# Agent attention and a tanh MLP on one core: the first keys with 49 agent columns, one weight quarter decoded later, two quarters split by ScalarE

## The chip, the cores and the metric

The kernel runs on one core of a Trainium2 chip. The metric is the device time of one execution in microseconds (us), lower is better. The core has TensorE (PE in the profile, with its weight loads as PEld), VectorE (DVE), ScalarE (ACT), GpSimd (POOL) and SyncE (SP), whose queue issues the DMAs here. Each works off its own instructions in order and waits for the others by semaphores.

## The reference

Per batch (4 batches, 12480 tokens, 128 channels) 49 agents attend to the keys and values, then the queries attend to the agents; the result goes through one MLP with `h - tanh(h)` between its two weights.

```python
def sm(a, b):
    s = scale * (a @ b.transpose(0, 2, 1))
    s = s - s.max(-1, keepdims=True)
    e = np.exp(s)
    return e / (e.sum(-1, keepdims=True) + 1e-09)
agent_v = sm(agents, k) @ v          # 49 x 128 per batch
x = sm(q, agents) @ agent_v          # 49920 x 128 in all
h = x @ w_in                         # w_in 128 x 2048
out = (h - np.tanh(h)) @ w_out       # w_out 2048 x 128
```

w_in and w_out come as float64; the kernel takes their bits as integers and makes float32 of them itself.

## The kernel before, in words

**Stages.** The 49920 tokens are cut into 100 blocks of 500, and each block passes eight steps (`HP = 8`, two 128-row chunks of the 2048 inner rows a step). One step is a first product `m1` (L563, into a PSUM tile `h`), `tanh` and `square` on ScalarE (L573, L578), the product `g` on VectorE (L583) and the second product `m2` (L632, into `acc`). For the 800 steps TensorE is the busy engine. In block 0 every step is "plain": `m2` multiplies by the float32 weights `wf` as they were decoded. From the third step of block 1 on most steps split `g` into a rounded part (GpSimd, L613) and a rest (VectorE, L618), and use W_out split in the same way, `wo_h` and `wo_l`.

**The opening** is what comes before block 0, and it is for batch 0 alone (`phase1(0)`; the other batches' attention is done between the steps of the blocks). In this order:

1. *Scores* (`scores`, L257): 13 groups of up to 8 key tiles. A key tile of 128 x 128 is the weight operand and the agents are the moving one (L273). The moving operand is `self.ag[:, 0:2, :]`: the 49 agents of batch 0 and the 49 of batch 1, 98 columns, of which only the first 49 of each tile are read afterwards. Eight tiles take two PSUM banks. ScalarE copies both halves to `s` (L284), VectorE takes a maximum over them (L286). After group 11 (`EARLY`) VectorE takes the maximum of what is there (L293), so that less is left at the end.
2. *Maximum* (L309 to L335): maximum over groups, a transpose on TensorE (L318), a second maximum, and a matmul with ones (L331) that spreads it to all partitions. Beside it TensorE makes the scores of the first queries (L508).
3. *Values* (`av`, L337): subtract the maximum (VectorE), exponential (ScalarE, L349), matmul with the values (L380); VectorE adds up the exponentials (L399). After the tenth group TensorE makes the transposes of the first query block (L538).
4. *Sums* (L391, `sums` at L408), then the projection `part` (L456): `av2` times w_in, in five column ranges (`PCUT`: 0, 256, 768, 1280, 1792, 2048), gives `awh` and `awl`, the weights of `m1`. The first two ranges are made ahead of block 0, the others at its steps 0, 2 and 4.

**Decoding.** Each of the two MLP weights comes in four quarters of 512 KB. `decode` (L167) makes one quarter: one ScalarE instruction (L174) and six of VectorE (L175, L177, L179, L181, L183, L185). The quarters of w_in are decoded during the scores, behind groups 3, 5, 7 and 9. Those of W_out are decoded from the sums on: quarter 0 ahead of block 0, the others in pairs of its steps, three VectorE instructions in the even step and three in the odd one. In block 0, VectorE's decodes of W_out carry the tile names `gh` and `gl`.

**Splitting W_out** (`split_w_out`, L208): per quarter GpSimd copies it rounded to `wo_h` (L213), subtracts for `wo_l` (L214), sets a column of ones (L215), and copies some plain pairs to `wo_f` (L218). `SPLIT = (8, 4, 6, 9)` puts quarter 1 at step 4 and quarter 2 at step 6 of block 0, quarters 0 and 3 at steps 0 and 1 of block 1.

**Order.** Loads go out on SP's queue in the order of the list `loads` (L716 to L725): keys, with a quarter of w_in ahead of groups 2, 4, 6 and 8; the first queries; values; quarters of W_out. Keys and values share 8 buffers (`K0`), and a value load waits for the keys that lay in its buffer. From the maximum on VectorE and ScalarE keep the order in which the code is written (`issue_order`); from `early` on TensorE and GpSimd do too.

Of the kernel before, what the change touches and what calls it, by code (L numbers as in the profile page):

```python
# [12 lines left out]
F32 = mybir.dt.float32  # L13
# [6 lines left out]
ALU = mybir.AluOpType  # L20
# [66 lines left out]
def run(job):  # L87
    for _ in job or ():
        pass
# [13 lines left out]
class Build:  # L103
# [94 lines left out]

    def load_w_in(self, c, raw):
        tiles = (self.work.tile([128, 512], F32, tag=t, name=t, bufs=2) for t in ("de", "rem", "da", "db"))  # L200
        run(self.decode(raw, self.w_in[:, c * 512 : (c + 1) * 512], *tiles))

    def load_w_out(self, c, raw):
        one, two = self.wtile("gl", NB["gl"]), self.wtile("gh", NB["gh"])
# [3 lines left out]
    def split_w_out(self, c):  # L208
        nc = self.nc
        w = self.wf[:, c * 512 : (c + 1) * 512]  # L210
        h = self.wo_h[:, 4 * c : 4 * c + 4, :].rearrange("p n e -> p (n e)")
        l = self.wo_l[:, 4 * c : 4 * c + 4, :].rearrange("p n e -> p (n e)")
        nc.gpsimd.tensor_scalar(h, w, 1.0, 0.0, ALU.mult, ALU.add)  # L213
        nc.gpsimd.tensor_tensor(l, w, h.bitcast(F32), ALU.subtract)  # L214
        nc.gpsimd.memset(self.vb[c][:, :, C : C + 1], 1.0)  # L215
        for i, t in self.wo_f.items():
            if c == i // 2:
                nc.gpsimd.tensor_scalar(t, w[:, 2 * C * (i % 2) :][:, : 2 * C], 1.0, 0.0, ALU.mult, ALU.add)  # L218

    def phase1(self, b):  # L220
        nc = self.nc
# [35 lines left out]
        def scores(g):  # L257
            yield
            if g == 0:
                st["s"] = self.keep.tile([128, NG * (GT + 1) * A], F32, tag="s", name="s", bufs=1)  # L260
                if b == 0:
                    st["mxp"] = self.work.tile([128, A, 2 * NG], F32, tag="mxp", name="mxp", bufs=1)
                else:
                    st["mxp"] = st["s"][:, NG * GT * A :][:, : A * NG].rearrange("p (a g) -> p a g", g=NG)
                st["acc"] = self.small.tile([128, C + 1], F32, tag="acc", name="acc")
            n = tiles(g)
            kt = ahead("k", load_k, g, 1 if b == 0 else kb)
            if b and g >= NG - vb:
                ahead("v", load_v, 0, g - NG + vb + 1)
            if b == 0:  # L270
                ps = self.banks("h")
                for t in range(n):
                    nc.tensor.matmul(  # L273
                        ps[:, t // 4, (t % 4) * A2 : (t % 4 + 1) * A2],
                        kt[:, t, :],
                        self.ag[:, 0:2, :],
                        start=True,
                        stop=True,
                    )
                pv = ps[:, :, : 4 * A2].rearrange("p c (t a) -> p c t a", a=A2)[:, :, :, :A]  # L280
                for c in range(-(-n // 4)):
                    m = min(4, n - 4 * c)
                    sl = slice((g * GT + 4 * c) * A, (g * GT + 4 * c + m) * A)
                    nc.scalar.copy(st["s"][:, sl].rearrange("p (t a) -> p t a", a=A), pv[:, c, :m])  # L284
                banks = -(-n // 4)
                nc.vector.tensor_reduce(  # L286
                    st["mxp"][:, :, 2 * g : 2 * g + banks].rearrange("p a c -> p c a"),
                    pv[:, :banks, : min(4, n)].rearrange("p c t a -> p c a t"),
                    axis=AX.X,
                    op=ALU.max,  # L290
                )
                if g == EARLY - 1:
                    nc.vector.tensor_reduce(  # L293
                        st["mxp"][:, :, 2 * NG - 1], st["mxp"][:, :, : 2 * EARLY], axis=AX.X, op=ALU.max
                    )
                return
            ps = self.misc()
            for t in range(n):
                for r in range(0, 128, QUART):
                    to = ps[r : r + QUART, t * A : (t + 1) * A]  # L300
                    nc.tensor.matmul(to, kt[:, t, r : r + QUART], self.ag[:, b, :], start=True, stop=True)  # L301
            yield
            here = st["s"][:, g * GT * A : (g * GT + n) * A]
            nc.scalar.copy(here, ps[:, : n * A])
            nc.vector.tensor_reduce(
                st["mxp"][:, :, g], here.rearrange("p (t a) -> p a t", a=A), axis=AX.X, op=ALU.max
            )

        def max_in():  # L309
            yield  # L310
            yield
            m = self.small.tile([128, A], F32, tag="m", name="m")
            part = st["mxp"] if b else st["mxp"][:, :, 2 * EARLY :]
            nc.vector.tensor_reduce(m, part, axis=AX.X, op=ALU.max)
            if b:
                yield
            ps = self.misc()
            nc.tensor.transpose(ps[:A, :128], m, self.ident)  # L318
            yield
            mc = self.small.tile([128, 1], F32, tag="mc", name="mc")  # L320
            nc.vector.tensor_reduce(mc[:A], ps[:A, :128], axis=AX.X, op=ALU.max)
            st["dg"] = self.small.tile([128, A], F32, tag="dg", name="dg")
            nc.vector.tensor_scalar(st["dg"][:A], self.ident[:A, :A], mc[:A], None, ALU.mult)
# [361 lines left out]
    def fast(self):  # L685
# [21 lines left out]
        with ExitStack() as first:  # L707
# [7 lines left out]
            self.wf = self.keep.tile([128, FF], F32R, tag="awh", name="awh", bufs=2).bitcast(F32)  # L715
            loads = []  # L716
            for g in range(NG):
                if g % 2 == 0 and 0 < g < 10:
                    loads.append((load_raw, g // 2 - 1))
                loads.append((self.k0, g))  # L720
            q1_load = lambda p: qt.update({p: self.q_load(q_src(p))})
            loads.append((q1_load, 0))
            for g in range(NG):
                loads.append((self.v0, g))
            loads += [(load_raw, 4), (q1_load, 1)] + [(load_raw, c) for c in (5, 6, 7)]  # L725
            free = K0
# [10 lines left out]
            for g in range(NG):  # L737
                run(p1[g])
                load(1)
                if g % 2 == 1 and 2 < g < 11:  # L740
                    self.load_w_in((g - 3) // 2, raws[(g - 3) // 2])
            at = self.count() - 1
            run(p1[NG])
            run(p1[NG + 1])
# [21 lines left out]
                load(1)  # L766
            for g in range(5, NG):
                run(av[g])
        early = self.count()
        self.main = ExitStack()  # L770
        self.begin(self.main, "main")
        for tag in ("y", "z", "g"):
            self.wtile(tag, NB[tag])
        dec = [self.load_w_out(c, raws[4 + c]) for c in range(4)]
        rest0 = p1[2 * NG + 3 :]
        sums = rest0.pop(0)
        q1 = q_job(1)
        next(q1)
        for _ in range(3):
            next(sums)  # L780
        next(q1)
        run(sums)
        part = rest0.pop(0)
        go(part, 3)
        go(dec[0], 3)
        run(part)
        next(q1)
        go(dec[0], 1)
        run(rest0.pop(0))
        run(dec[0])  # L790
        live = []
        kq = []
        r1, r2, done = [], [], []
# [60 lines left out]
        for k, (n, i) in enumerate(steps):  # L854
# [6 lines left out]
            if done and done[0][1] < k - 1:  # L861
                self.take(out_at(done[0][0]), acc[done[0][0]])
                finish(done.pop(0)[0])
            product(k)
            if n == LATE and i < NP:
                self.bound(0, i, slice(PCUT[i], PCUT[i + 1]))
            part = rest0.pop(0) if n == 0 and i in (0, 2, 4) else None
# [112 lines left out]
```

## Time and profile before

| | |
|---|---|
| median of 3 runs | 2017.74 us (2017.72 to 2019.99) |
| profiled execution, its own time | 2016.83 us |
| its span, first to last instruction | 2015.0 us |
| mean granted clock of TensorE | 0.997 |
| first key matmul starts | 5.62 us |
| first value matmul starts | 34.77 us |
| first projection matmul (L472) starts | 54.23 us |
| first product g (L583) starts | 59.10 us |

The page gives busy time per engine over the whole span, so its shares describe the 800 steps. For the opening the windows, the timeline and the chain of waits of the first 90 us are to be read. A timeline row is: start, length, engine, line, operation, output<-input, shapes, count, and in brackets the idle time before it with what ended it. Rows of one line that follow each other are merged, with their count. The granted clock of TensorE is given in each window as PEclk, 1.00 for full.

### The profile page before, as it was taken

To read this page: it belongs to the slowest core of one execution; us is meant where nothing else is said; L and a number is where in the kernel's file an instruction comes from. 1 tells how busy PE (TensorE), PEld (TensorE's weight loads), DVE (VectorE), ACT (ScalarE), POOL (GpSimd) and SP (SyncE) were. 2 spreads that over 40 slices of the span, in tenths; PEclk is the share of its full clock that TensorE was granted. 3 is DMA by queue.
4 is the path that set the end of the run, shared out by engine and by line. 5 is a ranking of instruction groups with operands and counts; after the bars stand their busy time and mean duration, and the time that the engine had idled before them with its cause. 6 is when DMAs were issued, how large, how long until landed. Compare 5 with 4: busy or idle time off the path is not lost.

```text
span 2015.0 us, 49566 instructions
## 1 busy us (share of the span) xinstructions
PE 1983.3 (98%) x20775; PEld 1464.4 (73%) x20775; DVE 1827.4 (91%) x1985; ACT 1804.1 (90%) x2044; POOL 1004.1 (50%) x709
## 2 busy tenths in 40 slices
PE   8899999999999999999999999999999999999998
PEld 7477777777677777777677777777777777777775
DVE  7899999889999998898999999889899999999997
ACT  3799989899999998899999999998999999999996
POOL 1344455555445455554454454555545546555553
PEclk9999999999999999999999999999999999999999
DMA  9322112221112222221112111221101101101100
GB/s 346 123 86 92 53 57 83 73 61 46 52 61 67 77 71 61 85 67 61 33 34 92 61 57 47 68 64 56 51 29 34 54 29 37 51 30 36 39 24 27
DMA packets 76744, 129.69 MB, mean 64 GB/s; under 512 B 5400, under 2 KB 55648, under 8 KB 76512
## 3 DMA queue, kind: packets, MB, share of 16 engines
q1 hardware_dynamic: 76512, 126.44, 19.1%
q8 instruction: 165, 2.70, 0.6%
q14 instruction: 67, 0.55, 0.1%
HBM read 81.10 MB, written 25.56 MB: 53 GB/s over the span
## 4 chain that ended last, share of the span: by engine, by line
PE 84%; ACT 9%; DVE 5%; issue 1%; DMA 0%; POOL 0%; SPq 0%; DVEq 0%; POOLq 0%
PE acc L632 49%; PE h L563 26%; ACT z L578 4%; ACT y L573 4%; DVE g L583 2%; PE misc L508 2%; PE misc L357 2%; PE pt L538 1%; PE misc L301 1%; PE h L273 1%; DVE gl L618 1%; PE misc L472 1%; ACT s L349 0%; DVE qe L524 0%; DVE s L344 0%
## 5 line engine op out<-in xcount | busy, mean ns | idle before, releaser
L613 POOL TENSOR_SCALAR gh<-g 128x1000 fp32r<-128x1000 f32 (+1 forms) x544 | 852.1, 1566 | 621.9 <-DVE g L583 578.3
L583 DVE TENSOR_TENSOR g<-h,z 128x1000 f32<-128x1000 f32 (+1 forms) x800 | 954.9, 1194 | 132.8 <-ACT z L578 121.8
L573 ACT ACTIVATE y<-h 128x1000 f32<-128x1000 f32 (+1 forms) x800 | 803.2, 1004 | 72.1 <-PE h L563 63.8
L578 ACT ACTIVATE z<-y 128x1000 f32<-128x1000 f32 (+1 forms) x800 | 831.3, 1039 | 25.4
L618 DVE TENSOR_TENSOR gl<-g,gh 128x1000 fp32r<-128x1000 f32 (+1 forms) x544 | 654.7, 1204 | 0.3
L563 PE MATMUL h<-pT,awh 49*128 49x504 f32 x1600 | 551.7, 424 | 0.0
L632 PE MATMUL acc<-g,wo_f 64*128 64x500 f32 (+1 forms) x1968 | 445.2, 578 | 0.0
L632 PE MATMUL acc<-gh,wo_l 64*128 64x500 f32 (+1 forms) x2176 | 433.0, 387 | 0.3 <-POOL gh L613 0.2
L632 PE MATMUL acc<-gh,wo_h 64*128 64x500 f32 (+1 forms) x2176 | 432.7, 386 | 0.0
L563 PE MATMUL h<-pT,awl 49*128 49x504 f32 x800 | 368.7, 461 | 10.3 <-DVE g L583 4.6
L632 PE MATMUL acc<-gl,wo_h 64*128 64x500 f32 (+1 forms) x2176 | 340.9, 387 | 1.0 <-DVE gl L618 0.5
L563 PE MATMUL h<-pb,awh 49*128 49x504 f32 x1600 | 317.4, 387 | 0.0
L563 PE MATMUL h<-pb,awl 49*128 49x504 f32 x800 | 309.0, 386 | 0.0
L632 PEld LDWEIGHTS acc<-g,wo_f 64*128 64x128 f32 x1968 | 192.6, 186 | 144.7 <-issue 126.2
L563 PEld LDWEIGHTS h<-pT,awh 49*128 49x128 f32 x1600 | 265.4, 186 | 19.5 <-issue 10.5
L632 PEld LDWEIGHTS acc<-gh,wo_h 64*128 64x128 f32 x2176 | 214.9, 186 | 36.2
L632 PEld LDWEIGHTS acc<-gl,wo_h 64*128 64x128 f32 x2176 | 212.1, 184 | 38.5 <-DVE gl L618 5.3
L632 PEld LDWEIGHTS acc<-gh,wo_l 64*128 64x128 f32 x2176 | 211.5, 184 | 37.1 <-POOL gh L613 1.1
L563 PEld LDWEIGHTS h<-pT,awl 49*128 49x128 f32 x800 | 147.4, 184 | 120.6 <-DVE o L641 49.1
L529 POOL TENSOR_TENSOR pp<-qe,pp 128x392 fp32r<-128x392 f32 x50 | 51.6, 1032 | 272.6 <-DVE pp L527 257.3
L563 PEld LDWEIGHTS h<-pb,awh 49*128 49x128 f32 x1600 | 154.6, 184 | 28.6
L563 PEld LDWEIGHTS h<-pb,awl 49*128 49x128 f32 x800 | 149.1, 186 | 12.4 <-issue 7.2
(113 smaller groups left out, 1130.0 us busy)
## 6 DMA issues: line engine op xcount, KB each, us to landing
kt<-kT SPq DMA_DIRECT2D x48, 512.0 KB
qt<-qT SPq DMA_DIRECT2D x46, 500.0 KB
outT<-o SPq DMA_DIRECT2D x46, 500.0 KB
pb<-pT SPq DMA_DIRECT2D x200, 96.5 KB
v<-v SPq DMA_DIRECT2D x36, 512.0 KB
vt<-v SPq DMA_DIRECT2D x12, 512.0 KB
raw<-w_in SPq DMA_DIRECT2D x4, 512.0 KB
v<-w_out SPq DMA_DIRECT2D x4, 512.0 KB
```

What stands on the lines that cost most here:

```text
L273: nc.tensor.matmul(ps[:, t // 4, (t % 4) * A2 : (t % 4 + 1) * A2], kt[:, t, :], self.ag[:, 0:2, :], start=True, stop=True,)
L301: nc.tensor.matmul(to, kt[:, t, r : r + QUART], self.ag[:, b, :], start=True, stop=True)
L357: nc.tensor.matmul(ps[HALF * odd : HALF * odd + w, : C + 1], flat[:r, t * A : t * A + w], vt[:r, t, : C + 1], start=t < 2, stop=t >= n - 2,)
L508: nc.tensor.matmul(to, qt[:, token : token + QUART], self.ag[:, b, :], start=True, stop=True)
L529: nc.gpsimd.tensor_tensor(pp[:, :, HALF:PW], ev, pp[:, :, :A].bitcast(F32), ALU.subtract)
L563: nc.tensor.matmul(h[:, c, : BT * TT], aw[a][rows[c], sl], pT[p][rows[c], :], start=k == 0, stop=k == 2)
L573: self.nc.scalar.activation(self.pair(y), h, AF.Tanh, scale=TSC)
L578: self.nc.scalar.activation(z, y, AF.Square, scale=GSC)
L583: self.nc.vector.tensor_tensor(self.pair(g), h, self.pair(z), ALU.mult)
L613: self.nc.gpsimd.tensor_scalar(gh, g, 1.0, 0.0, ALU.mult, ALU.add)
L618: self.nc.vector.tensor_tensor(gl, g, gh.bitcast(F32), ALU.subtract)
L632: nc.tensor.matmul(acc[:, r, :w], weights(c)[rows], g[rows, c * w : (c + 1) * w], start=i == 0 and k == 0, stop=i == NCH // 2 - 1 and k == ...
```

## The change

It does four things.

1. **Scores**: the moving operand is the 49 columns of batch 0 alone. Eight tiles then fit one PSUM bank (392 columns), with one ScalarE copy and one maximum of 392 elements per group. The array of maxima has 14 places instead of 26.
2. **w_in's fourth quarter** is loaded between the sixth and seventh group of values instead of among the keys, and decoded behind the sums, where W_out's quarter 0 was decoded. The first three quarters are decoded behind groups 3, 6 and 9, their loads go out ahead of key groups 2, 5 and 8.
3. **W_out's quarter 0** is decoded around the first product g: three VectorE instructions ahead of it, three behind it.
4. **W_out's quarters 1 and 2**: the rounded copy (and quarter 1's plain pair) is ScalarE's instead of GpSimd's. GpSimd's other plain copies are written as a copy instead of a multiply by one and an add.

The sums, the second query softmax and the first projections are written inside the first pool, as the decode of w_in needs its buffers.

```diff
-        run(self.decode(raw, self.w_in[:, c * 512 : (c + 1) * 512], *tiles))
+        return self.decode(raw, self.w_in[:, c * 512 : (c + 1) * 512], *tiles)
...
-        nc.gpsimd.tensor_scalar(h, w, 1.0, 0.0, ALU.mult, ALU.add)
+        if c in (1, 2):
+            nc.scalar.copy(h, w)
+        else:
+            nc.gpsimd.tensor_scalar(h, w, 1.0, 0.0, ALU.mult, ALU.add)
         nc.gpsimd.tensor_tensor(l, w, h.bitcast(F32), ALU.subtract)
...
-                nc.gpsimd.tensor_scalar(t, w[:, 2 * C * (i % 2) :][:, : 2 * C], 1.0, 0.0, ALU.mult, ALU.add)
+                on = nc.scalar.copy if c in (1, 2) else nc.gpsimd.tensor_copy
+                on(t, w[:, 2 * C * (i % 2) :][:, : 2 * C])
...
-                    st["mxp"] = self.work.tile([128, A, 2 * NG], F32, tag="mxp", name="mxp", bufs=1)
+                    st["mxp"] = self.work.tile([128, A, NG + 1], F32, tag="mxp", name="mxp", bufs=1)
...
-                ps = self.banks("h")
+                ps = self.misc()[:, : n * A]
                 for t in range(n):
-                    nc.tensor.matmul(
-                        ps[:, t // 4, (t % 4) * A2 : (t % 4 + 1) * A2],
-                        kt[:, t, :],
-                        self.ag[:, 0:2, :],
...
+                    nc.tensor.matmul(ps[:, t * A : (t + 1) * A], kt[:, t, :], self.ag[:, b, :], start=True, stop=True)
+                nc.scalar.copy(st["s"][:, g * GT * A : (g * GT + n) * A], ps)
...
                 if g == EARLY - 1:
...
+                    nc.vector.tensor_reduce(st["mxp"][:, :, NG], st["mxp"][:, :, :EARLY], axis=AX.X, op=ALU.max)
...
-                if g % 2 == 0 and 0 < g < 10:
-                    loads.append((load_raw, g // 2 - 1))
+                if g in (2, 5, 8):
+                    loads.append((load_raw, g // 3))
...
+                if g == 6:
+                    loads.append((load_raw, 3))
                 loads.append((self.v0, g))
...
-                if g % 2 == 1 and 2 < g < 11:
-                    self.load_w_in((g - 3) // 2, raws[(g - 3) // 2])
+                if g in (3, 6, 9):
+                    run(self.load_w_in(g // 3 - 1, raws[g // 3 - 1]))
...
+            part = rest0.pop(0)
+            go(part, 3)
+            w3 = self.load_w_in(3, raws[3])
+            go(w3, 3)
+            run(part)
+            next(q1)
+            go(w3, 1)
+            run(rest0.pop(0))
+            run(w3)
...
         go(dec[0], 3)
-        run(part)
-        next(q1)
-        go(dec[0], 1)
-        run(rest0.pop(0))
-        run(dec[0])
...
             product(k)
+            if k == 0:
+                run(dec[0])
```

Three places show what the change does to the order of the engines. (Names: `kt` keys, `ag` agents, `qt` queries, `v_90` to `v_93` the raw quarters 0 to 3 of W_out, `awh` on VectorE's and GpSimd's input side the decoded W_out, `awl` the rest of the projection.)

First TensorE at its start, before the change:

```order
L273 MATMUL h<-ag,kt 128x98 x98
L318 MATMUL misc<-ident,m 49x128
L331 MATMUL misc<-dg,ones 128x49
L508 MATMUL misc<-ag,qt_99 32x49 x32
L380 MATMUL h<-vt,s 64x128
```

and with it:

```order
L277 MATMUL misc<-ag,kt 128x49 x98
L306 MATMUL misc<-ident,m 49x128
L319 MATMUL misc<-dg,ones 128x49
L496 MATMUL misc<-ag,qt_99 32x49 x32
L368 MATMUL h<-vt,s 64x128
```

There are 98 matmuls as before, each with half the columns; the order is the same.

Then VectorE from the end of the sums to the second product g, before:

```order
L175 TENSOR_SCALAR gh<-v_90 128x512
L177 SCALAR_TENSOR_TENSOR gh<-v_90,gh 128x512
L179 TENSOR_SCALAR gh<-gh 128x512
L476 TENSOR_TENSOR awl<-h,awh 113x256
L515 TENSOR_REDUCE qm<-qe 128x8
L181 SCALAR_TENSOR_TENSOR gl<-v_90,gh 128x512
L476 TENSOR_TENSOR awl<-h,awh 113x512
L183 TENSOR_TENSOR gl<-gh,gl 128x512
L185 SCALAR_TENSOR_TENSOR awh<-gl 128x512
L583 TENSOR_TENSOR g<-h,z 128x1000
L476 TENSOR_TENSOR awl<-misc,awh 113x512
```

and with it, behind the first five instructions of that stretch (which make the same first half of a decode, the first part of `awl` and the maximum `qm`):

```order
L181 SCALAR_TENSOR_TENSOR rem<-raw,db 128x512
L464 TENSOR_TENSOR awl<-h,awh 113x512
L183 TENSOR_TENSOR rem<-da,rem 128x512
L185 SCALAR_TENSOR_TENSOR w_in<-de,rem 128x512
L175 TENSOR_SCALAR gh<-v_90 128x512
L177 SCALAR_TENSOR_TENSOR gh<-v_90,gh 128x512
L179 TENSOR_SCALAR gh<-gh 128x512
L571 TENSOR_TENSOR g<-h,z 128x1000
L181 SCALAR_TENSOR_TENSOR gl<-v_90,gh 128x512
L183 TENSOR_TENSOR gl<-gh,gl 128x512
L185 SCALAR_TENSOR_TENSOR awh<-gl 128x512
L464 TENSOR_TENSOR awl<-misc,awh 113x512
```

The six instructions of w_in's fourth quarter stand where W_out's quarter 0 stood, and that quarter's six stand around the first product g.

Last GpSimd at the split of W_out, before:

```order
L213 TENSOR_SCALAR wo_h<-awh 128x512
L214 TENSOR_TENSOR wo_l<-awh,wo_h 128x512
L215 MEMSET v_91 128x8
L218 TENSOR_SCALAR wo_f_88<-awh 128x256
L517 TENSOR_TENSOR qe<-qe,qm 128x392
L213 TENSOR_SCALAR wo_h<-awh 128x512
L214 TENSOR_TENSOR wo_l<-awh,wo_h 128x512
```

and with it, followed by ScalarE at the same steps:

```order
L217 TENSOR_TENSOR wo_l<-awh,wo_h 128x512
L218 MEMSET v_91 128x8
L505 TENSOR_TENSOR qe<-qe,qm 128x392
L217 TENSOR_TENSOR wo_l<-awh,wo_h 128x512
L218 MEMSET v_92 128x8
```

```order
L463 CAST awh<-misc 113x256
L214 CAST wo_h<-awh 128x512
L222 COPY wo_f_88<-awh 128x256
L561 ACTIVATE y<-h 128x1000
L566 ACTIVATE z<-y 128x1000
```

GpSimd's first subtraction now needs a result of ScalarE, whose cast stands behind the last cast of the projection (`awh<-misc 113x256`).

More of the change, by code (lines that the diff above doesn't have):

```diff
@@ L270, in scores @@
             if b == 0:
-                ps = self.banks("h")
+                ps = self.misc()[:, : n * A]
                 for t in range(n):
-                    nc.tensor.matmul(
-                        ps[:, t // 4, (t % 4) * A2 : (t % 4 + 1) * A2],
-                        kt[:, t, :],
-                        self.ag[:, 0:2, :],
[L277 to L285, printed above, removed]
+                    nc.tensor.matmul(ps[:, t * A : (t + 1) * A], kt[:, t, :], self.ag[:, b, :], start=True, stop=True)
+                nc.scalar.copy(st["s"][:, g * GT * A : (g * GT + n) * A], ps)
                 nc.vector.tensor_reduce(
[L287 to L290, printed above, removed]
+                    st["mxp"][:, :, g], ps.rearrange("p (t a) -> p a t", a=A), axis=AX.X, op=ALU.max
                 )
                 if g == EARLY - 1:
-                    nc.vector.tensor_reduce(
-                        st["mxp"][:, :, 2 * NG - 1], st["mxp"][:, :, : 2 * EARLY], axis=AX.X, op=ALU.max
-                    )
+                    nc.vector.tensor_reduce(st["mxp"][:, :, NG], st["mxp"][:, :, :EARLY], axis=AX.X, op=ALU.max)
                 return
@@ L312, in max_in @@
             m = self.small.tile([128, A], F32, tag="m", name="m")
-            part = st["mxp"] if b else st["mxp"][:, :, 2 * EARLY :]
+            part = st["mxp"] if b else st["mxp"][:, :, EARLY:]
             nc.vector.tensor_reduce(m, part, axis=AX.X, op=ALU.max)
@@ L768, in fast @@
                 run(av[g])
-        early = self.count()
+            early = self.count()
+            rest0 = p1[2 * NG + 3 :]
+            sums = rest0.pop(0)
+            q1 = q_job(1)
+            next(q1)
+            for _ in range(3):
+                next(sums)
+            next(q1)
+            run(sums)
+            part = rest0.pop(0)
[3 more added lines that the diff above has]
+            run(part)
+            next(q1)
+            go(w3, 1)
+            run(rest0.pop(0))
+            run(w3)
         self.main = ExitStack()
@@ L774, in fast @@
         dec = [self.load_w_out(c, raws[4 + c]) for c in range(4)]
-        rest0 = p1[2 * NG + 3 :]
-        sums = rest0.pop(0)
-        q1 = q_job(1)
-        next(q1)
[L779 to L784, printed above, removed]
-        go(dec[0], 3)
-        run(part)
-        next(q1)
-        go(dec[0], 1)
-        run(rest0.pop(0))
-        run(dec[0])
+        go(dec[0], 3)
         live = []
```

## The prediction

> **What bounds the kernel now.** I read the page first, then the windows of the opening, then single tiles and the chain.
>
> ```profile
> span 2015.0 us, 49566 instructions
> PE 1983.3 (98%) x20775; PEld 1464.4 (73%) x20775; DVE 1827.4 (91%) x1985; ACT 1804.1 (90%) x2044; POOL 1004.1 (50%) x709
> PE 84%; ACT 9%; DVE 5%; issue 1%; DMA 0%; POOL 0%; SPq 0%; DVEq 0%; POOLq 0%
> 600.00:1000.00 400.00, 399.14 (x4321) 291.06 (x4319) 365.41 (x394) 364.01 (x412) 203.63 (x143) 1.00 0.21 65
> ```
> From about 80 us on TensorE has no gap (399.14 of 400 us in the last row, a window of the steady part), and the change touches nothing there. So whatever the opening gains or loses before 80 us arrives unchanged at the end. All terms below are shifts of that point, made against the profiled execution (span 2015.0 us, its own time 2016.83 us); the median of the runs shown, 2017.74, lies 0.9 us above it.
>
> In the opening I ask who waits for whom, and at what pace the first scores (L273) run. The first two rows are from the waits of the first 60 us, the third from its groups; then come two answers on L273 alone (duration min/median/max in ns, first and last start), one timeline row, and one window of 1 us with the DMA rate in GB/s as its last number.
>
> ```profile
> ACT s L284 <- PE h L273: 13.5, 12, 2.0
> PE h L273 <- DMA kt<-kT: 5.6, 1, 5.6
> L273 PE MATMUL h<-ag,kt 128*128 128x98 f32 x196 | 24.7, 293 | 5.7 <-DMA kt<-kT 5.6
> L273 PE MATMUL h<-ag,kt x16: 421/421/421, 7.0 to 10.2; 128*128 128x98 f32 x16
> L273 PE MATMUL h<-ag,kt x92: 275/275/275, 11.8 to 21.9; 128*128 128x98 f32 x92
> 51.73 0.30 PEld L391 LDWEIGHTS h<-s,ones 128*128 128x128 f32 x2
> 12.00:13.00 1.00, 1.00 (x11) 1.00 (x11) 0.55 (x2) 0.99 (x3) 0.00 (x0) 1.00 1.00 410
> ```
> ScalarE waits for TensorE after every group, and TensorE waits for a load once, at the start: the scores are bound by TensorE. It makes 196 records (two for each of the 98 matmuls). Their spacing has two values: (10.2 - 7.0) / 15 = 213 ns before 10.7 us, and (21.9 - 11.8) / 91 = 111 ns after it. At the fast pace a group of eight matmuls takes 16 x 0.111 = 1.78 us; its 512 KB of keys need 0.524 / 410 GB/s = 1.28 us, so loads are not the limit.
>
> **Which part of a record sets this pace** decides what 49 columns bring. The L391 row has weights of 128 x 128 too, but 49 moving columns: two loads in 0.30 us, of which the last lasts about 0.19, so they too start 0.11 us apart. The pace is that of loading 128 columns of weights, whatever streams behind them. **Half the columns therefore saves nothing on TensorE.** It only halves the share of time in which columns stream.
>
> That share matters, because the granted clock follows it. These are windows of 3.41 us, laid so that each change of the clock falls on an edge (columns: length; busy us and instructions of PE, PEld, DVE, ACT, POOL; PEclk; DMA).
>
> ```profile
> 7.31:10.72 3.41, 3.41 (x18) 3.41 (x18) 2.33 (x5) 1.23 (x3) 0.00 (x0) 1.00 0.97 360
> 10.72:14.13 3.41, 3.41 (x33) 3.41 (x32) 2.72 (x6) 1.59 (x5) 0.00 (x0) 1.00 1.02 419
> 31.20:34.61 3.41, 1.50 (x67) 1.18 (x67) 2.27 (x7) 0.42 (x1) 0.00 (x0) 1.00 1.04 414
> 34.61:38.03 3.42, 3.26 (x32) 3.26 (x34) 2.45 (x5) 1.66 (x5) 1.09 (x1) 0.50 0.72 219
> 44.85:48.27 3.42, 2.14 (x39) 1.85 (x36) 3.42 (x6) 1.46 (x3) 1.12 (x1) 1.00 1.04 359
> 48.27:51.68 3.41, 3.41 (x28) 2.73 (x24) 1.97 (x4) 0.67 (x1) 0.00 (x0) 0.50 1.10 357
> 51.68:55.09 3.41, 2.94 (x75) 2.34 (x75) 2.34 (x8) 0.17 (x1) 0.00 (x0) 1.00 1.00 274
> 65.33:68.75 3.42, 1.74 (x12) 1.16 (x14) 3.38 (x4) 3.26 (x5) 2.73 (x5) 1.00 0.57 154
> 3.89:7.31 3.42, 1.69 (x8) 1.72 (x9) 1.00 1.02 361
> ```
> The clock is halved for one window after 31.20:34.61 and after 44.85:48.27, and the second pace of L273 (18 records touched, then 33) says that it was halved before 10.72 as well; the column shows 1.00 there only because no clock event was recorded before. Busy time is not what decides: 44.85:48.27 was busy for 2.14 us and lost the clock, 65.33:68.75 for 1.74 us and kept it. So I count streaming. The first two rows below are from the chain of waits, the others from the timeline.
>
> ```profile
> 80.00 1.68 PE acc L632 x8
> 81.67 0.69 PE h L563 x6
> 33.23 0.90 PE L508 MATMUL misc<-ag,qt 128*32 128x49 f32 x64
> 44.58 0.71 PE L380 MATMUL h<-vt,s 128*64 128x128 f32 x9
> 46.57 0.98 PE L538 MATMUL pt<-identr,pp 64*113 64x64 f32 x16 [1.28 <-POOL pp L529]
> 47.48 1.04 PE L380 MATMUL h<-vt,s 128*64 128x128 f32 x14
> ```
> Eight records of 500 columns, two side by side, take 1.68 us: 0.84 ns per column at full clock; the fp32r ones of L563 (three pairs of 504 in 0.69 us) 0.46 ns. My estimates from that: 98 columns stream 82 ns, 49 columns 41 ns, double at half clock.
> - 44.85:48.27: about 0.25 us of L380, 8 x 64 x 0.46 = 0.24 of L538, 7 x 0.107 = 0.75 of L380: share 0.36, clock lost.
> - 31.20:34.61: 16 x 41 ns (four of L508 side by side) and some 0.2 us of single ones: 0.25, lost.
> - 3.89:7.31: eight records of 165 ns: 0.38, stays halved.
> - 65.33:68.75: 0.69 us of L563 and about 0.9 of L632: 0.47, kept.
> - The scores now: 165 / 213 = 0.77 at half clock, which brought the full clock at 10.72; 82 / 111 = 0.74 after that.
>
> All windows up to 0.38 leave or put the clock at half, all from 0.47 leave it full. **With 49 columns the scores have 82 / 213 = 0.38 at half clock and 41 / 111 = 0.37 at full clock**: on the halved side both times. The second set of 49 columns, whose result is thrown away, was what kept the clock up.
>
> **The change, part by part.**
>
> 1. Scores at 49 columns. If the clock stays halved, all 196 records come 213 ns apart. They start at 5.6 us, when the first keys land, as now, so the last ends near 5.6 + 195 x 0.213 + 0.42 = 47.6 us; now it ends at 27.82 + 2.62 = 30.4 us (first row of the next fence): **+17.1 us**. (The other way round: some 24 records come at 213 ns today, 5.1 us, and 172 at 111; 172 x 0.102 = 17.5.) At full clock the term would be 0.
>
> 2. One PSUM bank, one copy, smaller maxima. ScalarE's one copy for two saves nothing: it waits for TensorE there. VectorE's tail is on the path:
>
> ```profile
> 27.82 2.62 PE L273 MATMUL h<-ag,kt 128*128 128x98 f32 x22
> 29.43 1.28 DVE L293 TENSOR_REDUCE mxp<-mxp 128x49 f32<-128x1078 f32 x1
> 30.62 0.73 DVE L286 TENSOR_REDUCE mxp<-h 128x98 f32<-128x392 f32 x2
> 31.38 0.36 DVE L314 TENSOR_REDUCE m<-mxp 128x49 f32<-128x196 f32 x1
> ```
> The early maximum reads 539 elements instead of 1078, so some 0.65 us, and the last two reductions no longer queue behind it: -0.5 us. Against that the few matmuls between the maximum and the values run at half clock in all cases but the full one: +0.3. The values' first windows run halved today too (34.61:38.03), so that is no new cost; as the edges of the clock's windows may fall elsewhere, 1.7 us either way stays open.
>
> 3. w_in's fourth part behind the sums. Its load (512 KB, 1.28 us at 410 GB/s) leaves the queue ahead of the last keys and stands behind six value loads; those wait for free buffers, not for the queue's rate, so nothing either way. Its decoding is six VectorE instructions and one of ScalarE. In the scores VectorE waits on TensorE anyway, so leaving saves nothing. Behind the sums it costs:
>
> ```profile
> 53.99 0.42 DVE L175 TENSOR_SCALAR gh<-v 128x512 uint32<-128x512 uint32 x1
> 54.45 0.69 DVE L177 SCALAR_TENSOR_TENSOR gh<-v,gh 128x512 uint32<-128x512 uint32 x1
> 66.87 1.38 DVE L175 TENSOR_SCALAR gh<-v 128x512 uint32<-128x512 uint32 x1
> 69.08 0.95 DVE L179 TENSOR_SCALAR gh<-gh 128x512 uint32<-128x512 uint32 x1
> 74.82 1.38 DVE L175 TENSOR_SCALAR gh<-v 128x512 uint32<-128x512 uint32 x1
> 77.23 1.43 DVE gh L179
> 66.64 1.28 POOL L214 TENSOR_TENSOR wo_l<-awh,wo_h 128x512 fp32r<-128x512 f32 x1
> 68.48 1.27 POOL L517 TENSOR_TENSOR qe<-qe,qm 128x392 f32<-128x392 f32 x1
> 55.78 0.59 ACT L475 CAST awh<-h 113x512 fp32r<-113x512 f32 x1
> 70.00:80.00 10.00, 6.84 (x38) 3.59 (x40) 9.86 (x12) 5.41 (x8) 5.24 (x8) 1.00 0.18 52
> ```
> From 54 to 79 us VectorE is the chain (9.86 of 10 us in the last row). Two of the six take 0.42, four about 0.69: 3.6 us, of which nothing is covered: +3.6. Behind it queue the products g, and TensorE waits for those.
>
> 4. Two quarters of W_out on ScalarE. Today four of VectorE's short instructions stand still while GpSimd works: L175 takes 1.38 us at 66.87, beside L214 (66.64 to 67.92), instead of 0.42; L179 at 69.08, beside L517, takes 0.95; the same again at 74.82 and 77.23. Excess: 0.96 + 0.53 + 0.96 + 1.0, about 3.5 us. After the change L214's work for the first quarter waits for ScalarE's cast, which stands behind awh's last cast, some 8 us later than now; the first pair then meets no GpSimd work and the second about half of it. I take -3.3 us; the bounds are 0 (the stalls only move) and -5 (all of them go, and the products too come closer together). ScalarE gets 2 x 0.59 and 0.37 us more, in a stretch where it is busy 5.41 of 10 us: hidden, or up to 0.6 us late for two tanh. Items 3 and 4 together: +0.3, between -1.5 and +4.
>
> Sum: 17.1 - 0.5 + 0.3 + 0.3 = 17.2 us; 2016.83 + 17.2 = 2034.0, and by the median 2034.9. I forecast **2034.5 us**.
>
> **Rivals.**
>
> *The clock is granted as now* (ends on the other side: not slower). The mechanism lies in the first two windows after 5.6 us: if the bound for the full clock is below a share of 0.37, or what counts is that the stream has no gaps, the records go to 111 ns at 10.7 us as before, term 1 is 0 and the rest is -0.2 to +0.3: 2017 us. For it speaks that 3.89:7.31, my nearest cold case, was filled only from 5.6 us on; against it 44.85:48.27, lost at 0.36 with two thirds of it busy. Chance 0.16. The Trainium skill, "TensorE: Matmul & The Clock Gate", Part 1, puts it that way: some 3.4 us of sustained matmuls bring the full clock and an idle window takes it. The trace agrees on the window (3.41 us) but not on the idleness: in 44.85:48.27 the longest gap was 1.28 us.
>
> *A bound between the two shares*, 0.37 and 0.38: full clock is granted and lost in turn, about half of term 1, some 2026 us. Chance 0.07.
>
> *The pace follows the columns after all*, if 111 ns is 82 of streaming and 29 beside it: 70 ns, 1.12 us a group, and the loads' 1.28 us would bind; the scores would end near 5.6 + 12.25 x 1.28 = 21.3 instead of 30.4 us: 2008 us. The L391 spacing of 0.11 us speaks against it. Chance 0.06.
>
> **How the numbers follow.** Chance of the forecast: 0.71. Its own range is 2030 (clock windows and stalls both in favour) to 2039 (items 3 and 4 at +4 us). To leave out no more than 2 in 10, the range reaches down to the case of the unchanged clock: 2016 to 2039. A measurement tells about 0.2%, 4 us, from no change: slower 0.77 (forecast, and the turn-taking clock), same 0.17, faster 0.06.
>
> **What would show it.** Right: the scores' records 213 ns apart to the end, ScalarE's copies 3.4 us apart, the score's last near 47 us, PEclk without a full event before the values; then VectorE's chain from the sums to 80 us as long as now, with short L175 in the third quarter. Wrong: copies 1.8 us apart (first rival), or mixed; a gap of 4 us more between the sums and the first dense block (items 3 and 4).

## The result, and the profile after

The changed kernel takes **2036.87 us** (median; 2036.47 to 2036.97), the kernel before 2018.05 us beside it: a ratio of 1.0092, 95% interval 1.008 to 1.0105. The profiled execution took 2036.79 us against 2016.83. The first two rows are from the page of after, and answer to those of before.

```profile
span 2035.0 us, 49544 instructions
PE 2003.0 (98%) x20775; PEld 1477.8 (73%) x20775; DVE 1827.2 (90%) x1985; ACT 1805.0 (89%) x2035; POOL 999.5 (49%) x706
```

TensorE is busy 19.7 us longer with as many instructions, and VectorE as long as before: something on TensorE runs slower. The next row is the answer on the line of the scores (L277 now): duration min/median/max in ns, first and last start in us.

```profile
L277 PE MATMUL misc<-ag,kt x196: 413/413/418, 5.3 to 46.9; 128*128 128x49 f32 x196
```

All 196 records have one length, and start (46.9 - 5.3) / 195 = 213 ns apart. In the kernel before only the first 24 or so did, and the rest came 111 ns apart. From the waits of the first 110 us of after (us in total, times, longest):

```profile
ACT s L278 <- PE misc L277: 30.6, 12, 2.9
PE misc L277 <- DMA kt<-kT: 5.3, 1, 5.3
PE h L551 <- DVE awl L464: 5.0, 4, 3.7
```

ScalarE waited 13.5 us for the scores before and waits 30.6 us now, and the keys are still waited for only once, at the start. The third row stood in the kernel before too (4.2 us, five times, at most 1.5); new is one wait of 3.7 us, behind the first product g. How the delay is carried on shows in TensorE's timeline:

```profile
48.41 0.42 PE L306 MATMUL misc<-ident,m 128*49 128x128 f32 x1 [1.06 <-DVE m L302]
51.73 10.00 PE L368 MATMUL h<-vt,s 128*64 128x128 f32 x160
71.23 1.51 PE L460 MATMUL h<-w_in,av 128*113 128x256 f32 x4
81.36 0.76 PE L551 MATMUL h<-pT,awl 49*128 49x504 f32 x1 [3.73 <-DVE awl L464]
```

The scores end at 46.94 + 0.41 = 47.35 us instead of 30.44 (+16.9), the first values start at 51.73 instead of 34.77 (+17.0), the first projection at 71.23 instead of 54.23 (+17.0). Between the scores and the projection nothing was gained or lost on balance. Behind it VectorE is the chain. These are rows of VectorE and GpSimd in the timeline of after, then those of before (L571 and L583 are the product g, L510 and L522 the same step of the query softmax):

```profile
82.65 1.19 DVE L571 TENSOR_TENSOR g<-h,z 128x1000 f32<-128x1000 f32 x1
86.99 0.42 DVE L175 TENSOR_SCALAR gh<-v 128x512 uint32<-128x512 uint32 x1
93.97 1.69 POOL L217 TENSOR_TENSOR wo_l<-awh,wo_h 128x512 fp32r<-128x512 f32 x1 [30.50 <-ACT wo_h L214]
94.56 1.43 DVE L179 TENSOR_SCALAR gh<-gh 128x512 uint32<-128x512 uint32 x1
99.39 2.30 DVE L571 TENSOR_TENSOR g<-h,z 128x1000 f32<-128x1000 f32 x2
100.03 1.28 POOL L217 TENSOR_TENSOR wo_l<-awh,wo_h 128x512 fp32r<-128x512 f32 x1 [3.34 <-ACT wo_h L214]
102.03 1.27 POOL L217 TENSOR_TENSOR wo_l<-awh,wo_h 128x512 fp32r<-128x512 f32 x1
102.19 1.18 DVE L510 TENSOR_SCALAR qs<-qs 128x8 f32<-128x8 f32 x1
103.64 0.79 DVE L512 TENSOR_TENSOR qe<-qe,qs 128x392 f32<-128x392 f32 x1
104.36 1.19 DVE L571 TENSOR_TENSOR g<-h,z 128x1000 f32<-128x1000 f32 x1
```

```profile
62.53 1.19 DVE L583 TENSOR_TENSOR g<-h,z 128x1000 f32<-128x1000 f32 x1
82.06 2.30 DVE L583 TENSOR_TENSOR g<-h,z 128x1000 f32<-128x1000 f32 x2
84.86 0.17 DVE L522 TENSOR_SCALAR qs<-qs 128x8 f32<-128x8 f32 x1
85.30 0.57 DVE L524 TENSOR_TENSOR qe<-qe,qs 128x392 f32<-128x392 f32 x1
85.79 1.19 DVE L583 TENSOR_TENSOR g<-h,z 128x1000 f32<-128x1000 f32 x1
```

Read the shifts of g from after minus before:
- second product (82.65 and 62.53): +20.1, so w_in's fourth quarter, decoded here, costs 20.1 - 17.0 = 3.1 us;
- the pair at 99.39 (82.06 before): +17.3, so 2.8 us are won back: L175 takes 0.42 us beside no GpSimd work where it took 1.38, and only one L179 (94.56) is still slow, beside L217;
- ninth product (104.36 and 85.79): +18.6. **1.2 us are lost anew:** GpSimd's subtraction for quarter 2 (100.03) now waits for ScalarE's cast, so its subtraction for quarter 0 behind it (102.03, at 76.74 before) meets the query softmax. The 128 x 8 step of that softmax takes 1.18 us instead of 0.17, and its last step, beside GpSimd's plain copies, 0.79 instead of 0.57.

Much later another 1.1 us is lost, at the 605th of the 800 steps, where a VectorE instruction again takes longer beside GpSimd's work. Two rows from the timelines of after, and VectorE's from that of before:

```profile
1570.47 2.03 POOL L601 TENSOR_SCALAR gh<-g 128x1000 fp32r<-128x1000 f32 x2 [1.04 <-DVE g L571]
1571.53 2.02 DVE L606 TENSOR_TENSOR gl<-g,gh 128x1000 fp32r<-128x1000 f32 x1 [0.35 <-POOL gh L601]
```

```profile
1552.38 1.20 DVE L618 TENSOR_TENSOR gl<-g,gh 128x1000 fp32r<-128x1000 f32 x1
```

With 0.3 us of drift the last product comes 20.0 us later than before: 17.0 + 3.1 - 2.8 + 1.2 + 1.1 + 0.3, rounded, which is the 19.96 us between the two profiled executions. The medians lie 18.8 us apart.

### The profile page after: what moved, and what is told of

The parts are those of the page before. It is cut to its first block, busy times and chain, and to the rows that moved or that the text cites. A ratio compares the mean times of both kernels' runs of the same rounds, so it can differ in the third digit from the quotient of the medians.

```text
span 2035.0 us, 49544 instructions
## 1 busy us (share of the span) xinstructions
PE 2003.0 (98%) x20775; PEld 1477.8 (73%) x20775; DVE 1827.2 (90%) x1985; ACT 1805.0 (89%) x2035; POOL 999.5 (49%) x706
## 4 chain that ended last, share of the span: by engine, by line
PE 83%; ACT 9%; DVE 6%; issue 1%; DMA 0%; POOL 0%; SPq 0%; DVEq 0%; ACTq 0%; POOLq 0%
PE acc L620 48%; PE h L551 26%; ACT z L566 4%; ACT y L561 4%; DVE g L571 3%; PE misc L277 2%; PE misc L496 2%; PE misc L345 2%; PE pt L526 1%; PE misc L289 1%; DVE gl L606 1%; PE misc L460 1%; ACT s L337 0%; DVE qe L512 0%; DVE qs L509 0%
## 5 line engine op out<-in xcount | busy, mean ns | idle before, releaser
L571 DVE TENSOR_TENSOR g<-h,z 128x1000 f32<-128x1000 f32 (+1 forms) x800 | 955.5, 1195 | 132.7 <-ACT z L566 121.7
```

Of the source, the lines that this page charges most:

```text
L571: self.nc.vector.tensor_tensor(self.pair(g), h, self.pair(z), ALU.mult)
```

## Experiments: is it the columns, and is it the clock?

My theory: the scores go at the pace of weight loads, and at half clock because 49 columns stream for too small a share of the time. The rival: something else of part 1 costs the time (one bank, one copy, the later order), or the columns never mattered. Every run from here on is compared with runs of the kernel before that were made beside it.

**49 columns alone.** The kernel before, with the moving operand cut and nothing else:

```diff
-                        self.ag[:, 0:2, :],
...
+                    to = ps[:, t // 4, (t % 4) * A2 : (t % 4) * A2 + A]
+                    nc.tensor.matmul(to, kt[:, t, :], self.ag[:, 0, :], start=True, stop=True)
```

> The kernel before, with the 49 columns of batch 0 alone as the moving operand of the scores and nothing else changed (same two banks, same copies, all four quarters of w_in among the scores). Theory (the share of time in which columns stream sets the granted clock; with 49 columns it is 0.38 at half clock and 0.37 at full clock, below the bound): the 196 score records come 213 ns apart to the end, the last near 47.5 us, and the time is 17 us above the kernel before, about 2035 us. Rival (the 19 us come from the parts behind the sums, or from the one bank with its single copy): within 1 us of the kernel before, about 2018 us.

Measured: 2034.62 us against 2017.15, ratio 1.0085 (1.0068 to 1.0102): +17.5. The source view of its score line:

```profile
L274 PE MATMUL h<-ag,kt x196: 413/413/421, 5.3 to 46.9; 128*128 128x49 f32 x196
```

The same 213 ns, and the first value starts at 51.72 us as with the whole change (51.73). The columns alone make the loss of the opening, in two banks with two copies as well; 17.5 of the 18.8 us are theirs.

**98 columns for the first four groups, 49 behind them.**

```diff
+                    to = ps[:, t // 4, (t % 4) * A2 :]
+                    if g < 4:
+                        nc.tensor.matmul(to[:, :A2], kt[:, t, :], self.ag[:, 0:2, :], start=True, stop=True)
+                    else:
+                        nc.tensor.matmul(to[:, :A], kt[:, t, :], self.ag[:, 0, :], start=True, stop=True)
```

> The kernel before with 98 moving columns in the first four groups of keys and 49 in the other nine. Theory: the full clock is granted at the edge of a window near 10.7 us as before, and lost at the edge behind the first window that holds only 49-column records (share 0.37). Of the 132 records at 49 columns all but the first 0 to 60 or so come 213 instead of 111 ns apart: 7 to 13.5 us above the kernel before, about 2025 to 2031 us. Rival (a high share is needed to get the clock, but a share of 0.37 without gaps keeps it): about 2018 us.

Measured: 2026.39 us, ratio 1.0043 (1.0026 to 1.006): +9.2. Windows of 3.41 us on the clock's edges (columns as in the prediction):

```profile
12.72:16.13 3.41, 3.41 (x34) 3.41 (x32) 3.34 (x8) 1.39 (x5) 0.00 (x0) 1.00 1.03 416
16.13:19.55 3.42, 3.42 (x33) 3.42 (x33) 2.90 (x6) 1.66 (x5) 0.00 (x0) 1.00 1.03 410
19.55:22.96 3.41, 3.41 (x18) 3.41 (x18) 3.31 (x8) 1.11 (x3) 0.00 (x0) 0.50 1.03 411
```

Here the clock was full, and it was lost behind a window in which TensorE is busy for all of 3.42 us, with 33 loads and 33 matmuls of 49 columns and no gap. This is the clearest row of the study: **it isn't idleness that costs the clock here, it is how little streams.** The Trainium skill, "TensorE: Matmul & The Clock Gate", Part 1, speaks of sustained matmuls and idle windows; by that rule this window would have kept the clock.

**How many columns bring the full clock?** The changed kernel with 56 and with 64 columns in its one bank, and the kernel before with 84 in two; all read only the 49 that are used.

The edit for 64, in part:

```diff
+                both = self.ag.rearrange("p b a -> p (b a)")[:, :64]
...
+                    nc.tensor.matmul(ps[:, t * 64 : (t + 1) * 64], kt[:, t, :], both, start=True, stop=True)
```

> The same with 56 moving columns: share 94/213 = 0.44 at half clock, 47/111 = 0.42 at full clock, between the largest share that lost the clock in the two traces (0.38) and the smallest that kept it (0.46). Theory: it tells on which side of 0.42 to 0.44 the bound lies: about 2019.5 us if the clock is granted and kept, about 2037 us if it never is, near 2028 us if it is granted and lost in turn. Rival (what counts is that the array is busy without gaps, by any share): 2037 us as with 49 columns, since the records' spacing is the same.

> The changed kernel with 64 moving columns (the 49 of batch 0 and 15 of batch 1), eight tiles of 64 filling one bank, still one copy and one maximum per group. Streaming share 108/213 = 0.50 at half clock and 54/111 = 0.48 at full clock. Theory: above the bound (windows from 0.47 on kept the clock), so the full clock is granted in the first full window and kept; 17 us less than the changed kernel, about 2019.5 us, that is 1 us above the kernel before (behind the sums the changed kernel loses some 1.5 us, the shorter maxima give 0.5 back). Rival (the grant needs a share above 0.5; the trace of before only shows grants at 0.77 and more): no change against the changed kernel, about 2037 us.

> The kernel before with 84 moving columns: streaming share 141 / 213 = 0.66 at half clock and 70 / 111 = 0.63 at full clock. If the full clock is given by a share of time a little over 0.5, it comes at the first full window as before and the time is that of before, 2017. If what counts is columns streamed in a window (98 columns at half clock are as many as 49 at full clock within 4%: 16 x 98 = 1568 against 30.7 x 49 = 1505), 84 columns give 1344 and the clock stays halved to the end of the scores: 2034. The two thirds of e8's first window, which did not bring it, speak for the second.

Measured: 2036.27 us with 56 (ratio 1.0092, 1.0075 to 1.0109), 2036.75 with 64 (1.01, 1.0083 to 1.0116), 2034.0 with 84 (1.008, 1.0066 to 1.0095). The first row is the source view of the score line with 64 columns, the second that with 84:

```profile
L278 PE MATMUL misc<-ag,kt x196: 421/421/443, 5.4 to 47.0; 128*128 128x64 f32 x196
```

```profile
L275 PE MATMUL h<-ag,kt x196: 420/421/478, 5.9 to 47.6; 128*128 128x84 f32 x196
```

None of the three left the slow pace during the scores. The theory for 64 columns missed by 17 us: my bound, 0.38 to 0.47, was wrong for a cold start. Shares of 0.50 and 0.66 at half clock do not bring the full clock, and 0.77 (98 columns) does, but only just. In the run with parts 3 and 4 of the next section, which has 98 columns, one window holds 16 of these records and is empty for its first 0.03 us; the full clock came only behind the next one:

```profile
5.85:9.27 3.42, 3.39 (x16) 3.42 (x17) 0.90 (x2) 0.69 (x1) 0.00 (x0) 1.00 1.00 351
9.27:12.68 3.41, 3.41 (x18) 3.41 (x18) 2.51 (x5) 0.55 (x2) 0.00 (x0) 1.00 1.03 420
```

Counted in columns instead of time, one bound would do for the scores: 16 x 98 = 1568 columns in a full window at half clock brought it, 16 x 84 = 1344 did not, and 3.41 / 0.111 = 30.7 records of 49, some 1505 columns, lost it at full clock. That agrees with these runs; none was made to tell it from two separate bounds for gaining and losing.

## Experiments: what w_in's fourth part and the splits cost

**Parts 3 and 4 with before's scores**, then the same with all four splits on GpSimd (part 3 alone), then with quarter 1 alone on ScalarE. (The parts are numbered as in the prediction; GpSimd's plain copies stay copies in all three.) The last one's edit against the first, its other line, the plain pair's, left out:

```diff
-        if c in (1, 2):
+        if c == 1:
             nc.scalar.copy(h, w)
```

> The changed kernel with the scores of the kernel before (98 columns, two banks, two copies, the long maxima); what is left of the change is w_in's fourth quarter behind the sums and the two quarters of W_out split by ScalarE. Theory (the clock cost 17 us, these parts the rest): full clock during the scores, and 1.5 us above the kernel before, about 2019.5 us, made up as in the trace of the changed kernel: up to 3 us late at the second product g, back to 0.3 at the sixth, and 1.2 more where the query softmax meets the second quarter's subtraction. Rival (the prediction's own term, +0.3): 2018.3 us. Second rival (these parts carry the loss): 2035 us or more.

> The kernel of the run with parts 3 and 4, with all four quarters of W_out split by GpSimd as in the kernel before; only w_in's fourth quarter behind the sums is left of the change. Theory (moving six VectorE instructions onto its own chain costs their 3.6 us, and GpSimd's work keeps stalling VectorE's short instructions): 3.6 us above the kernel before, about 2021.6 us; so the split by ScalarE gives back about 2 us. Rival (the stalls follow from where the instructions happen to meet, and the shift of 3.6 us takes some of them apart): 2019 to 2020 us, and the split by ScalarE is worth nothing.

> The kernel of the run with parts 3 and 4, with only quarter 1 split by ScalarE and quarter 2 by GpSimd. Theory (the last 1.2 us come from quarter 2's subtraction, which waits for ScalarE and then meets the query softmax on VectorE): that subtraction runs some 5 us earlier, between VectorE's decodes, and the time is 1.2 us below the run with both quarters, about 2018.3 us. Rival (the late 1.2 us have another cause): the same as with both, about 2019.5 us.

Measured against the kernel before: 2019.62 us (+2.1; ratio 1.0011, 1.0001 to 1.002), 2020.25 us (+2.8; 1.0015, 1.0005 to 1.0024), 2019.46 us (+2.0; 1.0009, 1.0 to 1.0018). By the medians the three can't be told apart. So the theories of the second (+3.6) and the third (1.2 us under the first) were not borne out; their rivals, 2019 to 2020 and about 2019.5 us, came closer. The timelines show what each does. VectorE with both splits on ScalarE, then with all on GpSimd, then with quarter 1 alone on ScalarE:

```profile
71.14 0.42 DVE L175 TENSOR_SCALAR gh<-v 128x512 uint32<-128x512 uint32 x1
78.71 1.43 DVE L179 TENSOR_SCALAR gh<-gh 128x512 uint32<-128x512 uint32 x1
86.34 1.18 DVE L526 TENSOR_SCALAR qs<-qs 128x8 f32<-128x8 f32 x1
```

```profile
70.33 1.37 DVE L175 TENSOR_SCALAR gh<-v 128x512 uint32<-128x512 uint32 x1
80.64 1.43 DVE L179 TENSOR_SCALAR gh<-gh 128x512 uint32<-128x512 uint32 x1
88.28 0.17 DVE L523 TENSOR_SCALAR qs<-qs 128x8 f32<-128x8 f32 x1
```

```profile
80.71 1.65 DVE L183 TENSOR_TENSOR gl<-gh,gl 128x512 f32<-128x512 f32 x1
86.09 0.17 DVE L526 TENSOR_SCALAR qs<-qs 128x8 f32<-128x8 f32 x1
```

In the first the softmax meets, as in after, quarter 0's subtraction, which quarter 2's pushed back. With the splits on GpSimd the decode's stalls are back (1.37) and the softmax's stall is gone (0.17): in these runs it was the one or the other. With quarter 1 alone on ScalarE the softmax is spared, but GpSimd's subtraction for quarter 2 (80.01 to 81.81) now lies beside L183, which takes 1.65 instead of 0.69. **A GpSimd subtraction moved by a few us moved the stall here, it didn't remove it.** The late 1.1 us is there, between the 604th and the 605th product g, in the traces of all seven kernels with a quarter on ScalarE and in none of the seven without; why the split of W_out reaches that far was not found out.

## Experiments: shorter weight loads

If 128-column loads set the pace, smaller weight operands that lie beside each other in the array should raise it, and keep 49 columns streaming for a larger share.

**Quarters of 32 columns**, in the changed kernel (with quarter 1 alone split by ScalarE):

```diff
-                    nc.tensor.matmul(ps[:, t * A : (t + 1) * A], kt[:, t, :], self.ag[:, b, :], start=True, stop=True)
+                    for r in range(0, 128, QUART):
+                        to = ps[r : r + QUART, t * A : (t + 1) * A]
+                        nc.tensor.matmul(to, kt[:, t, r : r + QUART], self.ag[:, b, :], start=True, stop=True)
```

> The changed kernel with each key tile loaded as four weight operands of 32 columns (as the other batches' scores do), 49 moving columns, one bank; and only quarter 1 of W_out split by ScalarE. Theory (the pace of the scores is that of loading 128 columns of weights in one piece; four pieces run side by side, as L508 shows with 64 records in 0.90 us): a group takes 0.7 us of TensorE at full and 1.4 at half clock, so loads and VectorE bind; with three quarters to decode VectorE ends the scores near 27 us instead of 30.4 before and 47.4 with the change; 3 us below the kernel before, about 2015 us. Rival (loads or VectorE bind the opening at its present length anyway): 2018 us.

Measured: 2025.96 us, ratio to before 1.004 (1.0026 to 1.0055): 11 us under the changed kernel, but 8.5 over the one before. TensorE's timeline of the scores:

```profile
20.07 2.83 PE L279 MATMUL misc<-ag,kt 128*32 128x49 f32 x127 [2.63 <-issue]
26.34 2.84 PE L279 MATMUL misc<-ag,kt 128*32 128x49 f32 x127 [3.44 <-issue]
30.54 2.83 PE L279 MATMUL misc<-ag,kt 128*32 128x49 f32 x127 [1.36 <-issue]
37.28 1.36 PE L279 MATMUL misc<-ag,kt 128*32 128x49 f32 x53 [3.91 <-issue]
```

The time expected was 2015 us. The bursts are as fast as hoped: 127 records in 2.83 us, 22 ns each, so 89 ns for the four that replace one of 213. But five times, most often behind some 127 records, TensorE stands for 1.4 to 3.9 us with nothing that the profile shows to wait for. These stops take 13 of the 33 us of the scores, and the full clock did not come during them. I took the stops for the supply of instructions, as there are four times as many. The DMA view counts seven packets of instructions on queue q8 (0.11 MB) in the first 45 us here, five with the halves below and three in the kernel before, but no run tested the cause by itself: it is not shown.

**Halves of 64 columns** have half of these instructions. In the kernel before, with 49 columns and with 98 (the expectations say "a tile" for one of a key tile's two passes):

```diff
+                    for r in (0, 64):
+                        to = ps[r : r + 64, t // 4, (t % 4) * A2 : (t % 4) * A2 + A]
+                        nc.tensor.matmul(to, kt[:, t, r : r + 64], self.ag[:, 0, :], start=True, stop=True)
```

> The kernel before, with 49 columns in the scores and each key tile as two weight operands of 64 columns, which stand in two halves of the array: 392 records instead of 196. In the run with quarters 127 records took 2.83 us, 22 ns each, that is 89 ns for a whole tile at half clock, but TensorE stood still for 1.4 to 3.9 us after every 127 or so, put down to issue. Theory (the streams are the pace once the weight loads lie side by side, and the instruction supply is what stopped the quarters): the halves also take some 90 ns for a tile at half clock, with a streaming share near 0.9, so the full clock comes in the first windows; the loads of 1.28 us a group are then the limit, less one stop of up to 3 us for each four groups: scores end at 22 to 28 us instead of 30.4, and what the values' loads leave of it at the end is 0 to 6 us: 2011 to 2018. Rival (halves load one behind the other, 213 ns for a tile at half clock): share 0.77 of streaming for the pair or less, scores end at 30 to 47 us, 2017 to 2034.

> The kernel before, 98 columns kept, each key tile as two weight operands of 64 columns. Theory as for 49 columns in halves: at half clock a tile takes the 165 ns of its 98 columns, share near 1, so the full clock is certain in the second window; then 82 ns for a tile against 111 now, 1.31 us a group, close to the loads' 1.28: scores end at 23 to 28 us, 2011 to 2018. Rival (loads one behind the other): 111 ns for a tile at full clock as now, scores end at 30 us, 2017.

Measured: **2014.01 us** with 49 and **2013.6 us** with 98, against 2017.67 before: both a ratio of 0.998 (0.9972 to 0.9989). TensorE's timeline with 49 columns, its waits, and the window that brought the clock:

```profile
5.43 3.66 PE L275 MATMUL h<-ag,kt 128*64 128x49 f32 x64 [5.43 <-DMA kt<-kT]
10.06 2.39 PE L275 MATMUL h<-ag,kt 128*64 128x49 f32 x64 [0.98 <-DMA kt<-kT]
30.50 0.28 PE L314 MATMUL misc<-ident,m 128*49 128x128 f32 x1 [2.46 <-DVE m L310]
33.38 10.46 PE L376 MATMUL h<-vt,s 128*64 128x128 f32 x160 [0.63 <-ACT s L345]
```

```profile
PE h L275 <- DMA kt<-kT: 10.2, 7, 5.4
```

```profile
5.80:9.21 3.41, 3.28 (x62) 3.12 (x59) 0.94 (x3) 1.32 (x4) 0.00 (x0) 1.00 1.00 317
```

A group of two (64 records) takes 3.66 us at half clock, 114 ns for a pair of halves instead of 213, and 2.39 us at full clock. Now TensorE waits for keys seven times (once at the start, as before): during the scores the loads are the bound, as the theory had it. So the gain is small. The scores end at 28.0 us instead of 30.4, and 1 us of that is lost again to VectorE, whose maxima now end later behind them (TensorE waits 2.46 us for `m` instead of 1.44): the values start at 33.38 instead of 34.77. The first products g lie 1.4 us earlier than before, the last one only 0.2 (0.9 and 1.1 with 98 columns), so it is not settled that the 3.7 us between the medians are the scores' (last section).

**Halves in the changed kernel**, which differs from it in this alone:

> The kernel after, with each key tile of the scores as two weight operands of 64 columns; nothing else differs from it. Theory (the loss is the 128-column weight loads at the halved clock, and the rest of the change costs about 2 us): the scores end near 28 us instead of 47, limited by the loads, as with the halves in the kernel before (2014.0 against 2017.7 there); with the 2 us that w_in's fourth part and the splits cost, less 0.5 us for the smaller maxima: 2015 to 2017, some 20 us under the kernel after. Rival (49 columns in one bank cost something of their own, by the one copy and maximum for a whole group, or the later decode costs more when the scores end early): 2019 or more.

Measured: 2015.11 us, ratio to before 0.9988 (0.9979 to 0.9997), 22 us under the changed kernel. TensorE's timeline:

```profile
24.63 2.31 PE L279 MATMUL misc<-ag,kt 128*64 128x49 f32 x72 [0.86 <-DVE mxp L281]
31.67 8.59 PE L370 MATMUL h<-vt,s 128*64 128x128 f32 x131 [0.16 <-ACT s L339]
```

The scores end near 27 us instead of 47. TensorE waits for the one bank once, 0.86 us for VectorE's maximum, and yet the values start at 31.67, earlier than with halves in the kernel before (33.38), where VectorE still has all of w_in to decode. So all of the loss but the 2 to 3 us of parts 3 and 4 lies in the pace of those loads. Halves in the kernel before have the lowest medians of the study, about 23 us under the kernel after.

## Why the prediction was right, point by point

- **What bounds the scores** (pace of 128-column loads, not columns): right. 49, 56, 64 and 84 columns all gave 213 ns, and shorter loads gave a faster pace.
- **Term 1, +17.1 us:** right, +16.9, by the mechanism named (records 213 ns apart to the end, last at 46.9).
- **Term 2, -0.5 and +0.3:** from the last score to the first value it is 4.38 us against 4.33, so 0 where the sum had -0.2: 0.4 us won up to the transpose behind the maximum (48.41), 0.4 lost behind it.
- **Items 3 and 4 together, +0.3: this term was mis-sized.** Each half was close (+3.1 for +3.6, -2.8 for -3.3), and up to the pair of products at 99 us their sum was what the prediction said. What was missing is what GpSimd's work, which the first pair of decodes no longer meets, would meet later: 1.2 us in the query softmax, and 1.1 us at step 605. The sum ended at 80 us, on the ground that the change touches nothing behind it; but with the change GpSimd's split of W_out lies from 94 us on, which is 77 in the time of before, and reaches past that point. By the run with these parts alone the two items cost 2.1 us, by the profiles of before and after 3, which is 1.8 to 2.7 more than the sum had. That accounts for the 2.4 us between the forecast, 2034.5, and the median. It stayed within the bounds that I had kept for them (-1.5 to +4).
- **The bound for the full clock, between 0.38 and 0.47:** wrong as a bound for gaining it, which took more than 0.66. The forecast hung on 0.38 being too little, and that was so by a wider margin than I knew: the first rival, the clock granted as now, deserved less than 0.16. The kernel before sat closer to the bound than the estimate of 0.77 told.
- The turn-taking clock did not appear, and the pace did not follow the columns: the other rivals fell by the same row.

## What to carry to other kernels

Where a stream of matmuls goes at the pace of its weight loads, cutting columns saved nothing here, and it took the clock away; count the columns that stream in each window, not the busy time. If the loads are the pace, try a narrower weight operand, in pieces that lie side by side, until something else binds, and watch the number of instructions. And when one engine's work is moved off another's short instructions, look up what runs at its new time.

## What the runs showed of the hardware

- The weight loads go at half pace too at half clock: 213 ns against 111 for the same 128 columns, so this stream, bound by them, ran at half pace as well.
- Two loads of 64 columns, in two halves of the array, take 114 ns at half clock where one of 128 takes 213: the two loads overlap.
- The changed kernel loses the clock again where TensorE waits 3.73 us for VectorE's `awl` (windows of after):

```profile
77.71:81.12 3.41, 0.00 (x0) 0.00 (x0) 3.34 (x5) 3.35 (x5) 0.00 (x0) 1.00 0.65 250
81.12:84.54 3.42, 3.18 (x12) 2.10 (x14) 3.32 (x7) 2.23 (x3) 0.00 (x0) 0.50 0.43 129
```

It costs nothing there: VectorE, busy for 3.32 of 3.42 us, is the chain, and the second and third product g lie equally late (+20.1).
- The very end differs between the programs. TensorE's last two semaphore instructions, in the source view of before and of the 49 columns in halves:

```profile
L976 PEldq EVENT_SEMAPHORE  x2: 51/51/51, 2014.7 to 2015.0; - x2
```

```profile
L972 PEldq EVENT_SEMAPHORE  x2: 51/51/51, 2012.3 to 2012.9; - x2
```

The last write is issued at almost the same time in both (2007.35 and 2007.13 us), and yet the first ends 2.1 us later; TensorE's first semaphore there comes 2.4 us later. So most of what the profiles show between these two lies behind the last write, and only 0.2 us ahead of it; the medians differ by 3.7 us. How much of that gain is the opening's, and how much the place at which TensorE's longer program ends, is not settled.
